# The last stores of a block-recurrent attention and MoE kernel: 64-row stores, and a last product in two column halves

## The chip, the cores and the metric

The kernel runs on one core of one Trainium2 chip. The time is the device time of one execution in microseconds (us). Three executions of the kernel before took 723.39, 723.47 and 724.16 us; their median, 723.47 us, is the time it is compared by.

A core has five engines with instruction streams of their own: TensorE (PE in the profile; PEld is its loading of weights), VectorE (DVE), ScalarE (ACT), GpSimd (POOL) and SyncE (SP). Transfers between the chip's memory (DRAM) and the on-chip memory are issued by SP, ACT or POOL and carried out by 16 DMA engines. PE accumulates into banks of PSUM, which DVE and ACT read.

## What is computed

```python
# x: (8, 8, 512, 64), state: (8, 8, 32, 64): batch, head, row, depth
a  = softmax(scale * x @ state.T);   xread = a  @ state      # 512 rows for each head
a2 = softmax(scale * state @ x.T);   sread = a2 @ x          # 32 rows for each head
y  = concat([xread, sread], axis=2)                          # (8, 8, 544, 64)
y  = y.transpose(0, 2, 1, 3).reshape(8 * 544, 8 * 64)        # (4352, 512)
h  = y @ w_in                                                # (4352, 2048)
sp = max(h, 0) + log1p(exp(-abs(h)))
out = (h * erf(sp)) @ w_out                                  # (4352, 512), float32
```

Every batch gives 544 rows of the output: 512 from `xread`, and then 32 from `sread`. So the `sread` rows of the eight batches lie in eight pieces of 32 rows, 544 rows apart.

## The kernel before

**Tiling.** The 512 `xread` rows of a batch are worked on together. The 32 `sread` rows of all eight batches are gathered into one more set of 256 rows, the last unit of work. Both dense products are done for blocks of two by two with seven products instead of eight (a Strassen-like scheme), so that a result is a sum of several products. `d_ff` is cut into four groups of 512, worked through in pairs.

**Order.** The first part of the kernel loads and converts the weights beside the first batch. A loop then runs over the other batches, two steps for each; in each step the second product of the step before (`project_wide`) is interleaved with the first product of this one (`hidden_wide`). After it comes the last unit (lines 1275 to 1295): two rounds of `hidden_states` and `project7`, which accumulate the 256 `sread` rows in the four PSUM tiles of `box`. The order of the instructions on PE, DVE and ACT is the order in which the code names them (`in_order`); SP takes its stores in the order in which it meets them.

**The last products (`project7`, lines 731 to 752).** Seven products, each of four matmuls of 128 rows by 128 by `E2` = 256 columns, go into the tiles `acc[0]` to `acc[3]`. In the trace, each float32 matmul leaves two records on PE. The seventh product goes into the left half of `acc[3]`.

**The last sums and stores (`store7`, lines 812 to 828).** ACT copies one half of a tile out of PSUM, DVE adds the halves of the others in five adds. `o1` holds the first 128 `sread` rows (batches 0 to 3), `o2` the other 128 (batches 4 to 7). Their stores follow as the parts become ready: the left half of `o1`, all of `o2`, and at last the right half of `o1`, which waits for the seventh product.

**The stores (`put_s`, lines 841 to 846).** Each call is cut into four stores of 32 rows, one for each batch:

```python
queue = nc.scalar if j % 2 and (r == 1 or c.start) else nc.sync
queue.dma_start(out=out[r0:r0 + Ns, c], in_=ot[Ns * j:Ns * j + Ns, c])
```

So the left half of `o1` goes by SP's queue alone, and the other two calls by SP and ACT in turn: 12 stores in all, eight on SP and four on ACT.

Of the kernel before, what the change touches and what calls it, by code (L numbers as in the profile page):

```python
# [17 lines left out]
def kernel(  # L18
# [17 lines left out]
    nc = tc.nc  # L36
    B, H, S, D = x.shape
    Ns = state.shape[2]
    d_model, d_ff = moe_w_in.shape
    P = 128  # L40
# [4 lines left out]
    GF = 4  # L45
    NG = NF // GF
    TB = S + Ns
# [66 lines left out]
    for i in range(NI):  # L114
        (nc.scalar, nc.sync)[i % 2].dma_start(
            out=x0[:, 2 * i:2 * i + 2].rearrange("p h c d -> p h (c d)"),
            in_=x[0, 2 * i:2 * i + 2].rearrange("h (p c) d -> p h (c d)", c=NC))
        if i == 1:
            for k in range(2):
                nc.sync.dma_start(out=st0[:, :, k],  # L120
                                  in_=state[0].rearrange("(g h) n d -> (h n) g d", g=2))
# [590 lines left out]
    E2 = d_model // 2  # L712
# [18 lines left out]
    def project7(gT, hs, g, first, last, acc, order=range(7)):  # L731


        blocks = lambda t: [t[:, k].rearrange("p (i t) -> p i t", i=GF) for k in range(4)]
        A11, A21, A12, A22 = blocks(gT)
        S1, S2, S3, S4 = blocks(hs)
        tt = nc.vector.tensor_tensor
        products = ((A12, B21, 0, 0), (A11, B11, 2, 0), (A22, T[4], 1, 0), (S2, T[2], 0, 1),
                    (S3, T[3], 2, 1), (S1, T[1], 1, 1), (S4, B22, 3, 0))
        for n, k in enumerate(order):  # L740
            lhs, rhs, bank, c = products[k]
            for i in range(GF):
                if i % 2 == 0 and n:
                    yield
                if i == 2 and n == 1:
                    tt(S1, A21, A22, op=ALU.add)
                    tt(S2, S1, A11, op=ALU.subtract)
                    tt(S3, A11, A21, op=ALU.subtract)
                    tt(S4, A12, S2, op=ALU.subtract)
                nc.tensor.matmul(out=acc[bank][:, E2 * c:E2 * c + E2], lhsT=lhs[:, i, :],  # L750
                                 rhs=rhs[:, g, i, :], start=(first and i == 0 and c == 0),
                                 stop=(last and i == GF - 1 and (c == 1 or bank == 3)))
# [59 lines left out]
    def store7(acc, put):  # L812
        twice = lambda t: t.unsqueeze(1).to_broadcast([P, 2, E2])
        two = lambda t: t.rearrange("p (c e) -> p c e", c=2)
        uv = outs.tile([P, d_model], F32, name="uv")
        m1, u3 = uv[:, 0:E2], uv[:, E2:]
        o1, o2 = (outs.tile([P, d_model], F32, name="ot", bufs=3) for _ in range(2))
        c12 = o1[:, E2:]
        add = lambda o, x, y: nc.vector.tensor_tensor(o, x, y, op=ALU.add)
        nc.scalar.copy(m1, acc[2][:, 0:E2])  # L820
        add(two(o1), twice(m1), two(acc[0]))
        put(0, o1, slice(0, E2))
        add(u3, c12, acc[2][:, E2:])
        add(two(o2), twice(u3), two(acc[1]))
        put(1, o2)
        add(c12, c12, acc[1][:, E2:])
        add(c12, c12, acc[3][:, 0:E2])
        put(0, o1, slice(E2, d_model))

    def put_x(b, h):  # L830
        rows = out[TB * b:TB * b + S].rearrange("(p c) e -> c p e" if b == 0 else
                                                "(c p) e -> c p e", p=P)

        def go(r, ot, c=slice(0, d_model), more=False):
            if more:
                nc.gpsimd.dma_start(out=rows[2 * h + r][:, c], in_=ot[:, c], accum_op=ALU.add)  # L836
            else:
                nc.sync.dma_start(out=rows[2 * h + r][:, c], in_=ot[:, c])
        return go

    def put_s(r, ot, c=slice(0, d_model)):
        m = P // Ns
        for j in range(m):
            r0 = TB * (m * r + j) + S
            queue = nc.scalar if j % 2 and (r == 1 or c.start) else nc.sync
            queue.dma_start(out=out[r0:r0 + Ns, c], in_=ot[Ns * j:Ns * j + Ns, c])

    def tiles(n):
        return [ps_o.tile([P, d_model], F32, name="o%d" % r) for r in range(n)]
# [108 lines left out]
    acc = tiles(NC)  # L958
# [114 lines left out]
    for u in range(2):  # L1073
        nc.sync.dma_start(out=kept_in[1][:, GF * u:GF * u + GF],
                          in_=away[:, u].rearrange("p j k f -> p j (k f)"))
# [71 lines left out]
    for n, (b, u) in enumerate((b, u) for b in range(1, B) for u in range(2)):  # L1147
# [3 lines left out]
        put = [put_x(b, h) for h in range(2)]  # L1151
# [124 lines left out]
    for k in range(2):  # L1276
        o = begins(B) ^ k
        steps = pending()
        if k == 0:
            later = combine_s(1 - begins(B))  # L1280
            steps = accompanied(steps, {1 + j: f for j, f in enumerate(later)})
        gT = hidden_states(o, 1 + k, lambda: next(steps, None))
        finish_on_act(gT[0])
        for j, _ in enumerate(steps):
            if j == (6 if k == 0 else 2):
                break
        times_part(1 + k, outside)
        times_part(1 + k, inside)
        done(steps)

        def pending(gT=gT, o=o, k=k):
            yield from project7(*gT, o, k == 0, k == 1, box)
            if k == 1:
                store7(box, put_s)
# [32 lines left out]
```

## Time and profile before

| | |
|---|---|
| median of three runs | 723.47 us |
| the profiled execution | 724.1 us |
| its span, first to last instruction | 722.3 us |
| PE busy | 714.6 us, 99% of the span |
| DVE, ACT, POOL busy | 538.2, 373.1, 25.2 us |
| DMA share from 714 to 718 us of the span | 0.09 |
| DMA share from 718 us to its end | 0.36 |
| mean rate of all transfers | 103 GB/s |

The profile is of one execution, whose own time lies a little above the median. The span leaves out what lies before the first and after the last instruction. A line of the timeline gives the start and duration in us, the engine, the line of the kernel, the operation, and the tiles written and read. Engines with a "q" (SPq, ACTq) are the instruction streams that issue transfers: such a row is the time of the issue, not of the transfer. A DMA share is the time in which the 16 DMA engines handled packets, over 16 times the stretch; a packet is a row of a transfer, or the few bytes that report its end. Where two packets overlap on an engine, both count.

### The profile page before, as it was taken

What the parts mean: (1) busy time and instruction counts of PE and PEld (TensorE: products, weight loads), DVE (VectorE), ACT (ScalarE), POOL (GpSimd) and SP (SyncE); (2) the same over time, 40 slices, a digit from 0 to 9 for tenths busy, and PEclk for the clock granted to TensorE, in tenths of its full rate; (3) what the DMA queues carried; (4) which work ended last, traced back from release to release, by engine and by line L of the source; (5) the groups of instructions that cost most, each with busy time, mean ns of one, the idle gap of its engine ahead of it and who ended that gap; (6) DMA issues with size and microseconds to landing.
All of it is one profiled execution on the core that took longest, in us unless ns stands there. A gap on an engine that the chain in (4) does not pass through costs nothing.

```text
span 722.3 us, 10976 instructions
## 1 busy us (share of the span) xinstructions
PE 714.6 (99%) x4289; PEld 565.5 (78%) x4289; DVE 538.2 (75%) x866; ACT 373.1 (52%) x540; POOL 25.2 (3%) x34
## 2 busy tenths in 40 slices
PE   9999999999999999999999999999999999999997
PEld 8444436588878878887888878887888888889996
DVE  5787879889868988788776967697877757665533
ACT  4999784636464625545346436462464535342340
POOL 0000000000100000000000000000000000000000
PEclk9999999999999999999999999999999999999999
DMA  8667795660348153513623280615242321002101
GB/s 266 193 220 211 231 273 180 148 178 30 46 89 217 21 130 55 140 51 92 98 29 147 59 140 8 175 28 148 31 103 84 89 49 27 33 29 30 24 8 30
DMA packets 144341, 74.73 MB, mean 103 GB/s; under 512 B 123424, under 2 KB 132896, under 8 KB 142752
## 3 DMA queue, kind: packets, MB, share of 16 engines
q1 hardware_dynamic: 139520, 65.95, 32.8%
q0 software_dynamic: 4032, 7.34, 7.5%
q10 hardware_dynamic: 736, 0.72, 0.3%
q8 instruction: 34, 0.56, 0.3%
q14 instruction: 19, 0.16, 0.1%
HBM read 49.87 MB, written 20.45 MB: 97 GB/s over the span
## 4 chain that ended last, share of the span: by engine, by line
PE 94%; ACT 3%; DMA 1%; DVE 0%; issue 0%; SPq 0%; ACTq 0%
PE o L775 47%; PE h L633 13%; PE at L633 10%; PE o L700 6%; PE h L678 3%; PE o L750 3%; PE h L905 2%; PE h L512 2%; PE at L512 2%; PE at L282 1%; PE h L232 1%; PE at L905 1%; PE at L529 1%; DMA x<-in_x_dram 1%; PE h L194 1%; PE at L329 1%
## 5 line engine op out<-in xcount | busy, mean ns | idle before, releaser
L775 PE MATMUL o<-w_out,ring 128*128 128x256 f32 x896 | 203.0, 379 | 0.0
L775 PEld LDWEIGHTS o<-w_out,ring 128*128 128x128 f32 x896 | 169.8, 190 | 25.0 <-DVE ring L1139 1.0
L775 PE MATMUL o<-raw,ring 128*128 128x256 f32 x672 | 161.4, 381 | 0.0
L775 PEld LDWEIGHTS o<-raw,ring 128*128 128x128 f32 x672 | 126.5, 190 | 25.9 <-ACT m L514 5.0
L626 ACT ACTIVATE ring<-ring 128x512 f32<-128x512 f32 x112 | 70.6, 631 | 59.9 <-DVE ring L616 59.3
L633 PE MATMUL h<-aT,m 128*128 128x256 f32 x336 | 82.0, 380 | 0.0
L1139 DVE TENSOR_TENSOR ring<-ring 128x1024 f32<-128x1024 f32 x60 | 70.6, 1218 | 3.9 <-ACT ring L690 3.9
L633 PEld LDWEIGHTS h<-aT,m 128*128 128x128 f32 x336 | 63.7, 190 | 10.4 <-issue 0.7
L616 DVE TENSOR_TENSOR ring<-ring,at 128x512 f32<-128x512 f32 x84 | 57.1, 680 | 16.9 <-PE at L633 15.2
L700 PE MATMUL o<-w_out,ring 128*128 128x512 f32 x128 | 58.8, 598 | 1.6 <-DVE ring L916 1.6
L760 DVE TENSOR_TENSOR ot<-uv,o 128x256 f32<-128x256 f32 (+1 forms) x56 | 30.9, 552 | 30.4 <-PE o L775 28.4
L616 DVE TENSOR_TENSOR ring<-ring,h 128x512 f32<-128x512 f32 x56 | 38.0, 678 | 19.7 <-PE h L633 19.6
L798 ACT COPY ot<-o 128x256 f32<-128x256 f32 x28 | 10.4, 373 | 79.6 <-PE o L775 79.6
L836 POOL DMA_DIRECT2D out_dram<-ot x28 | 24.5, 943 | 657.6 <-DVE ot L760 579.8
L700 PEld LDWEIGHTS o<-w_out,ring 128*128 128x128 f32 x128 | 23.7, 190 | 29.9 <-issue 24.4
L760 DVE TENSOR_TENSOR ot<-ot,o 128x256 f32<-128x256 f32 x56 | 22.1, 416 | 27.9 <-ACT ot L798 27.7
L648 ACT COPY ring<-h 128x512 f32<-128x512 f32 x28 | 16.5, 588 | 47.9 <-PE h L633 47.9
L807 DVE TENSOR_TENSOR ring<-ring 128x512 f32<-128x512 f32 x56 | 38.6, 689 | 1.4
L808 DVE TENSOR_TENSOR ring<-ring 128x512 f32<-128x512 f32 x56 | 36.3, 684 | 0.0
L639 ACT COPY ring<-h 128x512 f32<-128x512 f32 x28 | 16.5, 588 | 28.3 <-PE h L633 28.3
L690 ACT ACTIVATE ring<-ring 128x2048 f32<-128x2048 f32 x16 | 30.4, 1902 | 0.0
L514 ACT COPY m<-h 128x512 f32<-128x512 f32 x11 | 6.4, 586 | 44.4 <-PE h L512 44.3
(183 smaller groups left out, 975.6 us busy)
## 6 DMA issues: line engine op xcount, KB each, us to landing
w_in<-kept_in SPq DMA_DIRECT2D x7, 2048.0 KB, 8.2
raw<-in_moe_w_in_dram SPq DMA_DIRECT2D x16, 512.0 KB, 5.6
raw<-in_moe_w_out_dram SPq DMA_DIRECT2D x8, 1024.0 KB, 4.7
out_dram<-ot SPq DMA_DIRECT2D x32, 256.0 KB, 2.2
xq<-in_x_dram SPq DMA_DIRECT2D x112, 64.0 KB, 2.5
x<-in_x_dram SPq DMA_DIRECT2D x56, 128.0 KB, 2.9
out_dram<-ot POOLq DMA_DIRECT2D x28, 256.0 KB, 4.4
sc<-xT SPq DMA_DIRECT2D x112, 32.0 KB, 1.9
```

Of the source, the lines that this page charges most:

```text
L512: nc.tensor.matmul(out=ps[k][e][q, :], lhsT=st[r, b, q], rhs=of_group[g][r, :, i, :], start=True, stop=True)
L616: add = lambda o, x, y: nc.vector.tensor_tensor(o, x, y, op=ALU.add)
L626: nc.scalar.activation(out=s[k], in_=hs[k], func=ACTF.Softplus)
L633: nc.tensor.matmul(out=out[:, i], lhsT=x[:, q:q + P], rhs=y, start=(first and i == 0), stop=(i == 1), skip_group_check=not first)
L690: nc.scalar.activation(out=s, in_=s, func=ACTF.Erf)
L700: nc.tensor.matmul(out=acc[r], lhsT=gT[:, i, P * r:P * r + P], rhs=w_out[:, GF * g + i, :], start=(g == 0 and i == 0), stop=(g == NG - 1 a ...
L760: add = lambda o, x, y: tt(o, x, y, op=ALU.add)
L775: nc.tensor.matmul(out=out, lhsT=lhs[:, i, :], rhs=rhs[:, g, i, :], start=(start and i == 0), stop=(i == GF - 1), skip_group_check=not start)
L807: return [lambda: tt(S1, A21, A22, op=ALU.add), lambda: tt(S2, S1, A11, op=ALU.subtract), lambda: tt(S3, A11, A21, op=ALU.subtract), lambd ...
L808: lambda: tt(S3, A11, A21, op=ALU.subtract), lambda: tt(S4, A12, S2, op=ALU.subtract)]
L836: nc.gpsimd.dma_start(out=rows[2 * h + r][:, c], in_=ot[:, c], accum_op=ALU.add)
L1139: nc.vector.tensor_tensor(s[:, ks], s[:, ks], hs[:, ks], op=ALU.mult)
```

## The change

All of it is in the last unit. In `put_s` one store takes the rows of two batches: the DRAM side is viewed as batch, row, column, and SP takes the first two batches of a call and ACT the other two. Every call gives two stores of 64 rows instead of four of 32. In `project7` the seventh product is done for its left 128 columns and then for its right 128 columns, and in `store7` the last add and the last store are done for each of these halves by itself. That makes four calls of `put_s` instead of three, and eight stores instead of twelve, four on each queue.

```diff
@@ project7
             lhs, rhs, bank, c = products[k]
+            if last and n == 6:
+                yield
+                for q in range(0, E2, P):
+                    for i in range(GF):
+                        nc.tensor.matmul(out=acc[bank][:, q:q + P], lhsT=lhs[:, i, :],
+                                         rhs=rhs[:, g, i, q:q + P], start=False,
+                                         stop=(i == GF - 1 and q + P == E2))
+                break
             for i in range(GF):
@@ store7
         add(c12, c12, acc[1][:, E2:])
-        add(c12, c12, acc[3][:, 0:E2])
-        put(0, o1, slice(E2, d_model))
+        for q in range(0, E2, P):
+            add(c12[:, q:q + P], c12[:, q:q + P], acc[3][:, q:q + P])
+            put(0, o1, slice(E2 + q, E2 + q + P))
@@ put_s
-        m = P // Ns
-        for j in range(m):
-            r0 = TB * (m * r + j) + S
-            queue = nc.scalar if j % 2 and (r == 1 or c.start) else nc.sync
-            queue.dma_start(out=out[r0:r0 + Ns, c], in_=ot[Ns * j:Ns * j + Ns, c])
+        rows = out.rearrange("(b t) e -> b t e", t=TB)[:, S:TB, c]
+        for k, queue in enumerate((nc.sync, nc.scalar)):
+            b = P // Ns * r + 2 * k
+            queue.dma_start(out=rows[b:b + 2], in_=ot[2 * Ns * k:2 * Ns * k + 2 * Ns, c])
```

## The prediction

> **What bounds the kernel now.** I read the page first.
>
> ```profile
> span 722.3 us, 10976 instructions
> PE 714.6 (99%) x4289; PEld 565.5 (78%) x4289; DVE 538.2 (75%) x866; ACT 373.1 (52%) x540; POOL 25.2 (3%) x34
> PE 94%; ACT 3%; DMA 1%; DVE 0%; issue 0%; SPq 0%; ACTq 0%
> ```
>
> TensorE (PE) bounds the kernel: busy for 99% of the span and 94% of the chain that ended last. The change touches only what follows the last products, so I read the timeline of the end (start, duration, engine, line, work).
>
> ```profile
> 715.79 3.70 SPq L846 DMA_DIRECT2D out_dram<-ot  x8
> ...
> 716.19 1.89 PE L750 MATMUL o<-w_out,ring 128*128 128x256 f32 x8
> ...
> 717.00 0.41 DVE L819 TENSOR_TENSOR ot<-ot,o 128x256 f32<-128x256 f32 x1
> 717.11 2.34 ACTq L846 DMA_DIRECT2D out_dram<-ot  x4
> 718.12 0.42 DVE L819 TENSOR_TENSOR ot<-ot,o 128x256 f32<-128x256 f32 x1 [0.71 <-PE o L750]
> ```
>
> The last product is 8 records on PE, 716.19 to 718.08. The last add follows at 718.12 to 718.54. Twelve stores are issued between 715.79 and 719.5. From there only transfers stand between the kernel and its end. The issues of the stores, and a comparable issue elsewhere, are:
>
> ```profile
> L846 SPq DMA_DIRECT2D out_dram<-ot x8: 345/416/451, 715.8 to 719.1; - x8
> L846 ACTq DMA_DIRECT2D out_dram<-ot x4: 375/406/463, 717.1 to 719.0; - x4
> ...
> L484 SPq DMA_DIRECT2D sc<-xT x112: 586/608/1801, 116.2 to 565.0; - x112
> ```
>
> The middle figure is the median in ns. The last issues start at 719.0 and 719.1. In the DMA view of 718 to 722.3 us, the last of 22 occupied slices (0.1075 us each) ends at 720.4 us; the span ends 1.9 us later. In 716.6 to 717.2, the first packet is in the third slice of 15 ns, 716.63, so 0.84 us after the first issue began.
>
> **What a row costs a DMA engine.** The DMA views of four stretches: 716.6 to 718.0 (three 32-row stores), 646.8 to 648.4 (two stores with 2 KB rows), 9 to 11 (loads in 1 KB rows), 89 to 90 (loads in 256 B rows):
>
> ```profile
> DMA packets 145, 0.10 MB, mean 72 GB/s; under 512 B 48, under 2 KB 144, under 8 KB 145
> ...
> DMA packets 288, 0.52 MB, mean 328 GB/s; under 512 B 32, under 2 KB 32, under 8 KB 288
> q1 hardware_dynamic: 288, 0.52, 85.2%
> ...
> q1 hardware_dynamic: 731, 0.73, 104.5%
> ...
> q1 hardware_dynamic: 942, 0.23, 103.8%
> ```
>
> The last figure is the share of 16 engines' time. So 2 KB: 0.852 x 16 x 1.6 us / 256 rows = 85 ns. 1 KB: 1.045 x 16 x 2 us / 709 rows (22 of the 731 packets are under 512 B) = 47 ns. 256 B: 1.038 x 16 us / 942 = 17.6 ns. A 512 B row lies between; on the line from 256 B to 1 KB it is an estimated 27.5 ns.
>
> **What the Trainium skill says.** "DMA: Bandwidth & Descriptors", section "Why a DMA increments its semaphore by 16 and not by 1", says that a DMA is split over the largest number of engines, at most 16, that divides the slowest dimension of both its sides. On SP's and ACT's queues these are the lowest-numbered of the 16, and each posts one increment. Each 32-row store is 32 on both sides, so 16. The trace agrees: three such stores left 48 packets under 512 B, 16 each. No transfer here has a slowest dimension under 16, so the trace doesn't show what happens then. The section "Issuing engines are not separate DMA queues" says that SP's and ACT's transfers share the same engines; no view here tells the engines apart.
>
> **The change, part by part.**
>
> *Stores.* Each 64-row store has 64 partitions on the SBUF side, but on the DRAM side it is 2 batches x 32 rows x columns: its slowest dimension is 2, since rows of different batches are 544 rows apart. By that rule each store gets 2 engines, and all eight stores the same 2. The bytes don't change: 256 rows of 2 KB, 524 KB. Per engine:
>
> - left half, 128 rows of 1 KB: 64 x 47 = 3.0 us
> - full rows, 128 of 2 KB: 64 x 85 = 5.4 us
> - two quarters, 256 pieces of 512 B: 128 x 27.5 = 3.5 us
>
> Sum 12.0 us, where now the transfers fit into 716.63 to 720.4 and mostly wait for issues. These rows need no waiting: the left half is issued from 715.79, the full rows from 717.1 (to land after 717.9), the quarters before 719.7, and the first engine-time runs out only at 719.8 (left) and 725.3 (full). So two engines work without a gap.
>
> *Issues.* 12 become 8, four on each queue. I price one at 608 ns, the L484 row, instead of 416: both move several dimensions. That delays the first packet by 0.19, to 716.82. On ACT no computation follows its copy at 714.67, and on SP nothing but stores, so a longer issue holds up nothing else. Bounds: 416 (no delay) to twice 608 (0.8 us); the first packet moves with it.
>
> *Last product.* 8 matmuls of 128 columns instead of 4 of 256, 16 records instead of 8. L678 has this shape: 16 records in 1.95 us, the last 0.275, so 0.112 each from start to start, against 0.216 for 256 columns. The end is 716.19 + 15 x 0.112 + 0.275 = 718.14 instead of 718.08: +0.06, if weights load at L678's pace.
>
> *Last add.* The two halves each take an estimated 0.28 us (0.42 for 256 columns, 0.69 for 512, on a line), 0.14 more in sum. In the program as built, TensorE counts up once for these eight matmuls, at the last of them, and the first half's add waits for that count. So neither add starts before 718.18; they end at 718.46 and 718.74. Nothing is behind them on DVE. With two engines busy until 728.8, both parts are hidden by the transfers; without that cover they cost 0.2 us.
>
> *Sum.* The last packet ends at 716.82 + 12.0 = 728.8 instead of 720.4: +8.4. With the tail of 1.9 the span is 730.7. The profiled execution took 724.1, the median of the runs 723.47; I add the difference to the median: **731.9 us**, slower by 1.2%.
>
> Bounds of the rate: "DMA: Bandwidth & Descriptors", "Specifications", gives about 27 GiB/s (29 GB/s) per engine. By this estimate 262 KB per engine take 9.0 us, 728.9 in all; 2 KB rows ran at 24 GB/s here. For the other end I take the final stores themselves: from 716 to 722.3 the queues' shares are 17.7% and 12.4%, which is 0.301 x 16 x 6.3 = 30.3 engine-us for 524 KB, 17.3 GB/s, so 15.2 us and 735.1. That mixes both queues, as the changed kernel will; but each present store reads only 32 partitions with 16 engines, so I stay with the single-queue prices.
>
> **Rivals.**
>
> *Spread over 16 after all (not slower).* The hardware might split the 64 rows as it does 32 now. Then 24 engine-us divide by 16 and are hidden behind issues, as now. The adds release the last issues at 718.46 and 719.07 (the first takes 608), the last packets start 0.84 + 0.19 later, 720.1, and need 4 rows of 27.5 ns with some queueing: 720.3 against 720.4. Two issues fewer per queue are paid back by longer ones and by the shared wait: 723.4 us. It decides from 5 engines per store on: 24 / 5 = 4.8 us end at 721.6, less than 1.45 us above 720.4. For it: every transfer in the trace is spread so. Against it: none of them has a short outer dimension.
>
> *Two engines each, but different ones for SP and ACT.* Then 6.0 us from 716.82, 722.8, so +2.4: 725.9 us. Against it speaks the rule that both take the lowest-numbered.
>
> *A slower pair.* Two engines might not keep up their share-of-16 rate when two queues alternate on them: 735 us, the upper bound above, and more if each row waits for the last. For it: the 17.3 GB/s of the final stores. Against it: 24 GB/s in 646.8 to 648.4.
>
> **How the numbers follow.** Two shared engines 0.78 (forecast), the slower pair 0.07, different pairs 0.05, spread 0.10. The range 728.5 to 736.5 holds nearly all of the first and most of the second: 0.81. It reaches past the bounds by about what an issue of twice 608 adds (0.8). About 0.2% (1.45 us) is what a measurement of this kernel can tell from no change. The spread case lies within it, with a small chance of a gain beyond (0.02); the three others are slower.
>
> **What would show it.** Packets under 512 B in the last stretch fall from 192 to 16 (8 stores x 2); the DMA share there sits near 2 of 16 (12 to 13%) at about 45 GB/s for 12 us; the last issues start near 719.1 yet take some 9 us to land. Issues of 0.6 us, 16 records on PE ending at 718.14, and two adds back to back from 718.18 show the small parts. If the packets under 512 B number 128 and the last one falls before 721, the step on engines is wrong, and the time is no more than 723.9. If they number 16 and the transfers end far from 728.8, the price of a row is wrong.

## The result, and the profile after

The changed kernel took 733.36 us (median of 4), the kernel before 723.82 us (median of 4 with the new runs): 9.54 us more, a ratio of 1.0129 with a 95% interval of 1.0117 to 1.0141. The forecast was 731.9 us. The page of the profiled execution begins:

```profile
span 731.5 us, 10992 instructions
PE 714.2 (98%) x4297; PEld 565.5 (77%) x4297; DVE 538.1 (74%) x867; ACT 372.9 (51%) x540; POOL 25.2 (3%) x34
PE 93%; ACT 3%; DMA 1%; issue 0%; DVE 0%; SPq 0%; DVEq 0%; ACTq 0%
```

The engines did the same work as before, within 0.4 us each. The span is 9.2 us longer, and no engine is busy in the time that was added. The timeline of the end shows where computing stops:

```profile
714.86 0.69 DVE L827 TENSOR_TENSOR ot<-uv,o 128x512 f32<-128x512 f32 x1 [7.58 <-ACT uv L828]
715.58 3.84 SPq L854 DMA_DIRECT2D out_dram<-ot  x4
715.58 4.28 ACTq L854 DMA_DIRECT2D out_dram<-ot  x4
...
715.98 1.95 PE L746 MATMUL o<-w_out,ring 128*128 128x128 f32 x16
...
716.79 0.41 DVE L827 TENSOR_TENSOR ot<-ot,o 128x256 f32<-128x256 f32 x1
717.97 0.48 DVE L827 TENSOR_TENSOR ot<-ot,o 128x128 f32<-128x128 f32 x2 [0.76 <-PE o L746]
```

The last add ends at 718.45, where the kernel before ended it at 718.54. The last issues end at 719.4 (SP) and 719.9 (ACT). Everything after that is transfer. The issues, in ns (least, median, most):

```profile
L854 SPq DMA_DIRECT2D out_dram<-ot x4: 511/548/669, 715.6 to 718.9; - x4
L854 ACTq DMA_DIRECT2D out_dram<-ot x4: 522/742/1376, 715.6 to 719.3; - x4
```

And the DMA view of 716 to 731.5 us, in 40 slices of 0.39 us (share of the 16 engines in tenths, GB/s, packets):

```profile
DMA  0010111111120101111111111111111111100000
GB/s 0 0 16 18 48 24 24 40 42 37 40 53 24 16 37 32 53 53 53 48 48 53 53 50 46 52 53 42 45 42 45 42 44 44 30 9 0 0 0 0
DMA packets 528, 0.52 MB, mean 34 GB/s; under 512 B 16, under 2 KB 400, under 8 KB 528
```

The same count for the kernel before, from 716 to 722.3 us:

```profile
DMA packets 577, 0.53 MB, mean 85 GB/s; under 512 B 192, under 2 KB 448, under 8 KB 576
```

Two things are to be seen. The packets under 512 B, which report a store's end, are 16 for eight stores: two for each, where the kernel before had 192 for twelve, 16 for each. And the share stays near one tenth for 13 us, at some 50 GB/s in its best slices, where the kernel before moved the same bytes in 3.8 us. In the stretches of this time (the columns are busy us of each engine with its instructions, the granted clock, the DMA share, GB/s):

```profile
716.80:719.20 2.40, 1.13 (x11) 0.94 (x9) 0.89 (x4) 0.00 (x0) 0.00 (x0) 1.00 0.12 29
719.20:720.90 1.70, 0.00 (x0) 0.00 (x0) 0.00 (x0) 0.00 (x0) 0.00 (x0) 1.00 0.15 42
720.90:722.30 1.40, 0.00 (x0) 0.00 (x0) 0.00 (x0) 0.00 (x0) 0.00 (x0) 1.00 0.11 29
722.30:725.20 2.90, 0.00 (x0) 0.00 (x0) 0.00 (x0) 0.00 (x0) 0.00 (x0) 0.63 0.13 51
725.20:729.80 4.60, 0.00 (x0) 0.00 (x0) 0.00 (x0) 0.00 (x0) 0.00 (x0) 0.50 0.13 43
```

Two engines of 16, busy without a break, are a share of 0.125; packets that overlap on an engine, which both count, put it a little higher. The stretches lie at 0.11 to 0.15. The last packet ends at 729.75 (in the DMA view of 728 to 731.5 it is in the 20th slice of 0.0875 us), 1.8 us before the span ends.

### The profile page after: what moved, and what is told of

Its sections match the earlier page's. It is cut to its first block, busy times and chain, and to the rows that moved or that the text cites. A ratio compares the mean times of both kernels' runs of the same rounds, so it can differ in the third digit from the quotient of the medians.

```text
span 731.5 us, 10992 instructions
## 1 busy us (share of the span) xinstructions
PE 714.2 (98%) x4297; PEld 565.5 (77%) x4297; DVE 538.1 (74%) x867; ACT 372.9 (51%) x540; POOL 25.2 (3%) x34
## 4 chain that ended last, share of the span: by engine, by line
PE 93%; ACT 3%; DMA 1%; issue 0%; DVE 0%; SPq 0%; DVEq 0%; ACTq 0%
PE o L783 47%; PE h L633 13%; PE at L633 10%; PE o L700 6%; PE h L678 3%; PE o L758 3%; PE h L913 2%; PE h L512 2%; PE at L512 2%; PE at L282 1%; PE h L232 1%; PE at L913 1%; PE at L529 1%; DMA x<-in_x_dram 1%; PE h L194 1%; PE at L329 1%
```

## The experiments

The theory: a store whose DRAM side has 2 as its slowest dimension runs on two engines, and nothing else in the change costs much. The rivals: the halves of the last product and add; larger stores or the balance of the queues; a store whose two sides differ in form, whatever its slowest dimension. Each run is compared with runs of the kernel before on the same chip (medians 723.93, 724.26 and 724.08 us in three sets).

### Each part alone

**Stores alone.** The kernel before, with the new `put_s`.

> Only the stores are changed: 64 rows each, two batches to a queue; the last product, the last add and its store stay whole. Two engines for each store (the theory): per engine 128 rows of 1 KB and 64 of 2 KB, 128 x 46 + 64 x 84 ns = 11.3 us, against 64 x 46 + 64 x 84 + 128 x 27 = 11.8 us in the changed kernel, so 0.5 us less than that: about 732.9 us, and 12 packets under 512 B at the end (6 stores x 2). If the halves of the product and of the add are what costs (a rival), it is near the kernel before, 723 to 724.5 us.

Measured: 732.15 us, 1.0118 (1.0102 to 1.0133), 8.2 us over the kernel before. The last stretch, from 716 us, has

```profile
DMA packets 396, 0.52 MB, mean 36 GB/s; under 512 B 12, under 2 KB 268, under 8 KB 396
```

12 packets under 512 B for six stores, so two engines each. The stores alone make 8.2 of 9.5 us. Against the changed kernel that is 1.3 us less, where 0.5 was expected. From the start of the last sums to the last packet the two profiles have 14.9 and 14.5 us, so 0.4 of it lies there; the rest stays open.

**Halves alone.** The changed kernel, with the `put_s` of the kernel before.

> Only the halves are changed: last product, last add and last store in two halves, with the stores of the kernel before (32 rows, its choice of queue), 16 in all. Two engines for each 64-row store (the theory): the loss is gone; SP issues ten stores, its last at about 719.7 instead of 719.1, so 0.4 to 0.8 us over the kernel before, about 724.2 us. If the halves cost (a rival): 732 to 734 us.

Measured: 724.79 us, 1.0012 (1.0005 to 1.0018), 0.9 us over, a little more than the 0.4 to 0.8 that were expected. The halves aren't what costs; the 16 stores are a small loss of their own. The rival falls.

### The same stores, cut or reordered

**Stores of 32 rows.** Halves, queues, bytes and row sizes of the changed kernel; only each store is cut in two.

```diff
-        rows = out.rearrange("(b t) e -> b t e", t=TB)[:, S:TB, c]
         for k, queue in enumerate((nc.sync, nc.scalar)):
-            b = P // Ns * r + 2 * k
-            queue.dma_start(out=rows[b:b + 2], in_=ot[2 * Ns * k:2 * Ns * k + 2 * Ns, c])
+            for j in (2 * k, 2 * k + 1):
+                r0 = TB * (P // Ns * r + j) + S
+                queue.dma_start(out=out[r0:r0 + Ns, c], in_=ot[Ns * j:Ns * j + Ns, c])
```

> The changed kernel with each 64-row store cut into two of 32 rows on the same queue: same halves, same queues, same bytes and row sizes, 16 stores of 16 engines. Two engines (the theory): 0.4 to 0.8 us over the kernel before, 724.2 us, last packet near 721.0, 256 packets under 512 B. If the size of the last pieces or the balance of the two queues costs (a rival): near 733 us.

Measured: 724.85 us, 1.0012 (1.0006 to 1.0019), 0.9 us over, again a little more than expected. Twice as many issues take away 8.6 of the 9.5 us. Small last pieces and the balance of the queues fall as causes.

**Slowest dimension 16.** The rows of each half of the last unit are ordered by row and then batch. That is done where the `sread` columns are written to `sT`, so no work is added.

```diff
-    sT = const.tile([P, NK, B, Ns], F32, name="sT")
+    sT = const.tile([P, NK, 2, Ns, 4], F32, name="sT")
...
-        rows = out.rearrange("(b t) e -> b t e", t=TB)[:, S:TB, c]
+        rows = out.rearrange("(b t) e -> t b e", t=TB)[S:TB, 4 * r:4 * r + 4, c]
         for k, queue in enumerate((nc.sync, nc.scalar)):
-            b = P // Ns * r + 2 * k
-            queue.dma_start(out=rows[b:b + 2], in_=ot[2 * Ns * k:2 * Ns * k + 2 * Ns, c])
+            t = Ns // 2 * k
+            queue.dma_start(out=rows[t:t + Ns // 2], in_=ot[2 * Ns * k:2 * Ns * k + 2 * Ns, c])
```

> The changed kernel, with the 128 rows of each half of the last unit ordered by row and then batch instead of batch and then row. A store still takes 64 rows, on the same queues, in eight issues, and its two sides still differ in form (64 partitions against 16 x 4 rows), but the slowest dimension of the DRAM side is 16 instead of 2. Two engines (the theory): 16 engines, 128 packets under 512 B, last packet near 720.4, 723.4 us or within 0.4 us of the kernel before. If a store whose sides differ in form is slow in itself (a rival), or if 64-row stores are: 731 to 734 us.

Measured: 724.04 us, 1.0003 (0.9994 to 1.0011), 0.1 us over. The DMA view of 716 to 721.9 us (slices of 0.15 us):

```profile
DMA  0046661000149997510052613343000000000000
GB/s 0 0 160 222 236 236 35 0 0 0 69 181 292 347 333 278 222 56 0 0 167 70 181 28 118 105 132 91 0 0 0 0 0 0 0 0 0 0 0 0
DMA packets 640, 0.52 MB, mean 89 GB/s; under 512 B 128, under 2 KB 512, under 8 KB 640
```

Eight stores of 64 rows on the same queues, two sides that still differ in form, and 128 packets under 512 B: 16 for each. The transfers come in three bursts with gaps, up to 347 GB/s, waiting for issues again. So it is the slowest dimension of the DRAM side that costs, and neither 64 rows nor the form. This is the run that settles the cause.

**Slowest dimension 4.** One store of 128 rows for each call, all on SP.

```diff
-        for k, queue in enumerate((nc.sync, nc.scalar)):
-            b = P // Ns * r + 2 * k
-            queue.dma_start(out=rows[b:b + 2], in_=ot[2 * Ns * k:2 * Ns * k + 2 * Ns, c])
+        b = P // Ns * r
+        nc.sync.dma_start(out=rows[b:b + 4], in_=ot[:, c])
```

> The changed kernel with one store of 128 rows for each call, all on SP: 4 stores, DRAM side 4 batches x 32 rows. By the theory each gets 4 engines: half the transfer time of the changed kernel, 6.0 us by the prices of the prediction and 6.5 us by what the changed kernel measured, so a last packet 6.0 to 6.5 us after the first, 2.4 to 3.0 us over the kernel before (about 726.6 us), 16 packets under 512 B. If every store whose sides differ in form ran on two engines (a rival): 733 us again. If nothing but the count of issues mattered: below the kernel before.

Measured: 728.38 us, 1.0053 (1.0039 to 1.0066), 4.1 us over: more than was expected, and 16 packets under 512 B for four stores, so four engines each. The count, and the stretches of its end:

```profile
DMA packets 529, 0.53 MB, mean 27 GB/s; under 512 B 16, under 2 KB 400, under 8 KB 528
...
717.00:718.80 1.80, 1.14 (x11) 0.95 (x9) 0.90 (x4) 0.00 (x0) 0.00 (x0) 1.00 0.24 72
718.80:720.00 1.20, 0.00 (x0) 0.00 (x0) 0.00 (x0) 0.00 (x0) 0.00 (x0) 1.00 0.28 25
720.00:722.50 2.50, 0.00 (x0) 0.00 (x0) 0.00 (x0) 0.00 (x0) 0.00 (x0) 1.00 0.22 72
722.50:725.10 2.60, 0.00 (x0) 0.00 (x0) 0.00 (x0) 0.00 (x0) 0.00 (x0) 0.65 0.23 71
```

A share of about a quarter is four engines. In the last stretch they moved the 256 pieces of the quarters and the last 26 full rows: 256 x 27.5 + 26 x 85 ns are 9.3 engine-us at the forecast's prices, and four engines took 2.5 us, 10.0 engine-us. Before it they were slower than their prices: 72 in the first stretch (1 KB rows, 4 x 1024 / 47 = 87) and in the third (2 KB rows, 96), and only 25 for 1.2 us at the start of the full rows. At a share of 0.28 the engines weren't idle then; the rows took longer. In the trace's records of single packets, 19 of the 128 rows of 2 KB took 144 to 853 ns, the median 84. With four engines the loss is less than half of that with two, in the direction of the theory, but not to its number. The run also has one queue and half the issues, so the dimension isn't all that it changes.

**Slowest dimension 8.** The order of the rows of the run with 16, in stores of 8 x 4 rows, two on each queue for each call.

```diff
-            t = Ns // 2 * k
-            queue.dma_start(out=rows[t:t + Ns // 2], in_=ot[2 * Ns * k:2 * Ns * k + 2 * Ns, c])
+            for t in (Ns // 2 * k, Ns // 2 * k + Ns // 4):
+                queue.dma_start(out=rows[t:t + Ns // 4], in_=ot[4 * t:4 * t + Ns, c])
```

> The rows of the last unit ordered by row and then batch, as in the run with outermost dimension 16, but in stores of 8 x 4 rows, two on each queue for each call: 16 stores, outermost dimension 8. By the theory 8 engines each: 24 engine-us over 8 are 3.0 us, hidden behind the issues (the point of decision was put at 5 engines), so 0.3 to 1.0 us over the kernel before for the 16 issues, like the run with 16 stores of 32 rows; 128 packets under 512 B. If each halving of the engines cost in proportion even here (a rival): over 726 us.

Measured: 727.39 us, 1.0043 (1.0029 to 1.0056), 3.1 us over. By the time alone, the rival of a cost in proportion would have won. Its last stretch has 8 packets under 512 B for each store, and the issues, here and in the run with 16 stores of 32 rows, say otherwise:

```profile
DMA packets 641, 0.53 MB, mean 56 GB/s; under 512 B 128, under 2 KB 512, under 8 KB 640
```

```profile
L854 SPq DMA_DIRECT2D out_dram<-ot x8: 657/688/814, 716.1 to 721.5; - x8
L854 ACTq DMA_DIRECT2D out_dram<-ot x8: 671/672/1521, 716.1 to 722.1; - x8
```

```profile
L854 SPq DMA_DIRECT2D out_dram<-ot x8: 314/398/414, 715.6 to 719.6; - x8
L854 ACTq DMA_DIRECT2D out_dram<-ot x8: 374/405/447, 715.6 to 719.6; - x8
```

Eight issues of 0.69 us on a queue last 5.5 us; eight of 0.40 last 3.2. The last issue starts at 721.5 and 722.1 instead of 719.6, 1.9 and 2.5 later, or 1.4 and 2.0 when the later start of 0.5 is taken off. The queues' shares in this run's last stretch (716 to 725.6) are 8.0% and 7.9%, so transfers were waiting for issues: from its first packet to its last, 6.1 us, no packet was in flight for some 2.5 us. The expectation had priced 16 issues of this form like those of plain stores. So here most of the loss is a price of the issue. It doesn't show what eight engines cost.

### The two queues, and what the forecast missed

**One queue.** All eight stores on SP: `(nc.sync, nc.sync)` in place of `(nc.sync, nc.scalar)`.

> The changed kernel with all eight stores on SP, none on ACT. The two engines are the same for either queue (the theory): the transfers take as long, 12.0 to 13.0 us, and the time is within 1 us of the changed kernel, 732.5 to 733.8 us. If the 0.9 us by which the changed kernel's transfers exceeded the forecast came from two queues alternating on an engine: 12.0 us, 732.5. If it comes from the start of a transfer on two engines: 13 us again, 733.4. If ACT had had engines of its own (a rival): at least 4 us more than the changed kernel.

Measured: 734.36 us, 1.0137 (1.0122 to 1.0153), 10.1 us over, 0.6 above what the changed kernel was over. The median missed the range of the expectation by 0.6 us, over a kernel before that was itself 0.4 us slower in this set. The rates from 717 to 731 us (slices of 0.35 us):

```profile
GB/s 0 18 6 44 53 47 35 18 47 50 47 35 23 29 41 47 41 53 53 47 41 59 47 53 53 47 54 38 39 28 35 41 44 44 44 34 22 22 22 1
```

Without ACT's queue the transfers took 13.3 us (717.4 to 730.7), 12.9 with it. ACT has no engines of its own for these stores, and the excess over the forecast doesn't come from two queues alternating.

**Queues exchanged.** ACT takes the first two batches of each call, SP the others (one execution with its profile).

> The changed kernel with the queues exchanged: ACT takes the first two batches of each call and SP the other two. The same bytes on the same two engines (the theory): 733 to 734 us, first to last packet 12.5 to 13.5 us. For what the forecast missed, the low rate of the first microseconds on two engines: if it belongs to SP's queue, the rows of SP stay slow and ACT's are as fast as before; if it belongs to whichever store comes first on the two engines, the first 2.4 us stay near 30 GB/s whichever queue carries them.

Measured: 733.68 us, against 724.28 for the kernel before, each from one execution. In both kernels, the stretch of 716.8 to 719.2 carried SP's rows alone or nearly so, at 29 and 26 GB/s (the changed kernel, then the exchanged one):

```profile
q1 hardware_dynamic: 66, 0.07, 12.1%
q10 hardware_dynamic: 3, 0.00, 0.4%
```

```profile
q1 hardware_dynamic: 60, 0.06, 11.0%
```

So the slow rows are not a matter of which batches are written. SP's rows came first in both, although ACT's first store was issued within 0.01 us of SP's. That leaves SP's queue and the place of the first store untold apart.

**Full rows alone, quarters alone, on two engines.** The run with stores of 32 rows, with the new form only for the full rows (`if r == 1`) or only for the two quarters (`if c.start`).

> The run with 16 stores of 32 rows, but with the two stores of the full rows (batches 4 to 7) in the form of the changed kernel, 64 rows and outermost dimension 2. Two engines (the theory): 64 rows of 2 KB on each, 5.4 us at 84 ns, from a first packet about 0.9 us after the issue at 717.1: last packet near 723.3 to 723.6, 2.9 to 3.2 us over the kernel before. If the 0.9 us that the changed kernel took beyond the forecast belongs to the first microseconds of any work on two engines, it comes again here: 3.9 us over. If it belongs to the left half alone, it does not.

> The same with only the four stores of the two quarters in the form of the changed kernel. Two engines (the theory): 128 rows of 512 B on each, 3.5 us at 27 ns, from a first packet at 719.4: last packet near 722.9, 2.5 us over the kernel before; with a slow start of 1 us, 3.5 us over. If the parts didn't add up on the same two engines, the sum of this and of the run with only the full rows would not come near the changed kernel's 9.5 us less the 3.0 us of the left half.

Measured: quarters 726.68 us, 1.0036 (1.0022 to 1.0050), 2.6 us over, as expected without a slow start. There is hardly one in its rates from 718.9 to 722.6 us (slices of 0.09 us):

```profile
GB/s 0 17 11 17 39 44 39 44 44 44 44 44 44 44 44 33 44 44 44 44 33 22 39 44 44 44 39 44 44 44 44 39 44 44 44 39 22 11 0 0
```

The full rows 729.86 us, 1.0080 (1.0062 to 1.0098), 5.8 us over, where at most 3.9 was expected. The timeline and the stretches of that kernel show two things that go with it:

```profile
718.49 5.32 SPq L860 DMA_DIRECT2D out_dram<-ot  x4
```

```profile
718.40:720.00 1.60, 0.00 (x0) 0.00 (x0) 0.26 (x2) 0.00 (x0) 0.00 (x0) 1.00 0.12 16
```

Four plain stores behind the full rows on SP were issued in 5.32 us instead of 1.6: they were held up behind a store that fills two engines. Not every issue is: in the changed kernel, where each store behind the first had such a store ahead of it, none on SP took over 0.6 us. What decides it isn't shown. And the first 1.6 us of the two engines moved 16 GB/s at a share of 0.12: they were busy, and slow. The slow start comes again without the left half on two engines, so it doesn't belong to that half; without it in the quarters, it doesn't belong to every transfer on two engines either. The parts don't add: 5.8 + 2.6 is already 8.4, and the left half is still missing. Some of it is counted twice, since both runs also have plain stores for the rest, and 16 plain stores alone are 0.9 us over.

### A version for use

**Slowest dimension 16, with the last product, add and store whole.**

> The rows of the last unit ordered by row and then batch, stores of 64 rows with outermost dimension 16, one on each queue for each call, and the last product, add and store whole as in the kernel before: 6 stores instead of 12. The last issues start at about 718.6 instead of 719.1, each 0.6 us long instead of 0.4: last packet at 720.0 to 720.2, 0.1 to 0.5 us below the kernel before, a ratio of 0.9993 to 1.0, too little to tell from it by the time. If 64-row stores or stores whose sides differ cost something of their own (a rival): 0.5 us or more over the kernel before.

Measured: 723.74 us, 0.9993 (0.9984 to 1.0001). The last issue starts at 718.6, 0.5 us before that of the kernel before, as expected. But the last packet ends at 720.4, as there: the DMA view of 716 to 721.7 us (slices of 0.14 us) has the last burst from 719.7 on, 1.1 us after the issue.

```profile
DMA  0000000266630000368989554026763000000000
```

It halves the stores and loses nothing; a gain can't be told from no change.

## Why the prediction was right

**Engines for each store: right.** Two packets under 512 B for each, at a share of 0.11 to 0.15. The run with slowest dimension 16 shows it as the cause: same rows, issues and halves, and 9.4 of 9.5 us gone. In the runs the count of these packets was 2, 4, 8 and 16 for slowest dimensions of 2, 4, 8 and 16, as the Trainium skill has it ("DMA: Bandwidth & Descriptors", "Why a DMA increments its semaphore by 16 and not by 1"). The records of single packets say it a second way. Leaving out the few ns by which a row overlaps the next, never more than two packets were in flight at once at the end of the changed kernel and of the runs with the stores alone and with one queue, and never more than 4, 8 and 16 with slowest dimensions of 4, 8 and 16. The trace of before couldn't show that.

**Both queues on the same two engines: right.** From 722.4 to 725.0 both queues moved rows, at shares of 7.5% and 5.5%: two engines of 16 in sum, where four would show 25%. One queue alone took 13.3 us for the transfers, two took 12.9.

**The price of a row: too high once the transfer ran, too low at its start.** From 722.4 to 725.0 the changed kernel moved 64 packets of 2 KB, and from 727.3 to 729, 143 rows of 512 B and four small packets:

```profile
DMA packets 64, 0.13 MB, mean 50 GB/s; under 512 B 0, under 2 KB 0, under 8 KB 64
q1 hardware_dynamic: 37, 0.08, 7.5%
q10 hardware_dynamic: 27, 0.06, 5.5%
...
DMA packets 147, 0.07 MB, mean 43 GB/s; under 512 B 4, under 2 KB 147, under 8 KB 147
q1 hardware_dynamic: 74, 0.04, 7.2%
q10 hardware_dynamic: 73, 0.04, 7.1%
```

By the shares, as the forecast reckoned, a 2 KB row took 0.13 x 16 x 2.6 us / 64 = 84.5 ns, against 85, and a 512 B row 27.2, against the 27.5 interpolated. But where packets overlap on an engine, a share counts both. By the clock, each of the two engines moved a 2 KB row every 2 x 2.6 us / 64 = 81 ns and a 512 B row every 2 x 1.7 us / 143 = 24 ns. For 1 KB rows the records of single packets have 42 ns from one start to the next where no row was slow. At these prices the sum would have been 64 x 42 + 64 x 81 + 128 x 24 ns = 10.9 us instead of 12.0.

Slow single rows, which the forecast had at nothing, went the other way. In the records, 16 of the 128 rows of 1 KB took 101 to 281 ns instead of 46, and four of the 128 rows of 2 KB took 341 to 539 ns instead of 84; none of 512 B did. All twenty started before 722, and what they took beyond the others is 3.4 engine-us, 1.7 us for two engines. So the 67 rows of 1 KB from 716.8 to 719.2 took 2 x 2.4 us / 67 = 72 ns on average, and the left half was through at 720.9, 4.0 us after the first packet, instead of 3.0.

All of it took 12.9 us from first to last packet, instead of 12.0: 1.1 us less by the prices, 1.7 more by the slow rows, and 0.3 that no term explains. The number of engines was understood; that the sum came so close was in part luck, since two errors went opposite ways. The excess of 0.9 us is most of the 1.1 us by which 9.54 exceeds 8.4.

**The start: 0.2 us short.** From the first issue at 715.58 to the first packet at 716.85 are 1.27 us, against 0.84 + 0.19. The issue was priced by its median, 608 ns instead of 416. But SP's first issue took 0.67 us, and that of the kernel before 0.34: 0.33 more, not 0.19. That is 0.14 of what was missed; the other 0.1 lies between the end of the issue and the first packet.

**The sum.** The profiled execution began its last sums at 714.86, 0.21 earlier than the kernel before. From there to the last packet are 14.9 us, against 5.4 (715.07 to 720.43): 9.5, the difference of the medians. With the forecast's terms it was 8.4; the longer transfers are 0.9 and the first packet 0.2.

**The product in halves, and the shared wait: right.** 16 records in 1.95 us, as in L678. Both adds came after the whole product (0.76 us of idle time ended by PE), so the first half started nothing early. Their 0.48 us are less than the estimated 0.56. All of it was hidden by the transfers; with the transfers on 16 engines, the halves and their 16 stores cost 0.9 us.

**The rivals.** A spread over 16 engines would have given 723.4; the run that brought it about by the order of the rows gave 724.04 on a chip where the kernel before took 723.93. (The working of this rival has two issues fewer for each queue; SP has four fewer, and ACT as many as before.) Different engines for the two queues fell. The slower pair was right about a low rate at the start (29 GB/s until 719.2 and again from 720.9 to 722.3), but not about its reason: in both stretches SP's rows went almost alone, and where the queues alternated the rate was 51 GB/s.

**The point of decision, at five engines, wasn't confirmed.** Four engines cost 4.1 us where 2.4 had followed from it, since slow rows are there as well; eight engines were never the bound in the run meant for them.

## What to carry to other kernels

Before rows of several pieces are put into one store to save issues, look at the slowest dimension on both sides: a store with 2 there ran on two of 16 engines and turned 3.8 us of transfers into 12.9, and nothing at a kernel's end hides that. If the pieces must go together, order the data on chip so that the long dimension is the slowest on the DRAM side too (9.4 of 9.5 us came back). And an add or a store cut in half starts nothing early unless what it waits for is counted half by half.

## What was not expected

- On two or four engines some rows were slow, nearly all in the first microseconds of the left half or the full rows (with one queue a few until 727): 29 GB/s in the first 2.4 us and 51 later with two, 25 GB/s for 1.2 us at the start of the full rows with four, 16 GB/s in the first 1.6 us of the full rows alone. The engines count as busy meanwhile. With the quarters alone it lasted only 0.3 us. With 16 engines the burst of the left half is at 222 GB/s in its second slice of 0.15 us. The cause stays open. Which batches are written and alternating queues are excluded. Of the twenty slow rows of the changed kernel 18 were SP's, but SP's rows also came first in each of these calls, so SP's queue and the first place aren't told apart.
- With two stores issued within 0.01 us on SP and ACT for the same two engines, ACT's rows began only when SP's were through: 3 packets of ACT before 719.2, 49 from 719.2 to 720.4. From 723.3 on the records show rows of the two queues in turn on both engines. ACT's longest issue took 1.38 us, SP's 0.67.
- An issue of a store whose sides differ in form took 0.54 to 0.69 us on SP (medians of the runs), of a plain one 0.40 to 0.42. With eight of 0.69 on a queue, the issues took 5.5 us, and the transfers of all 16 stores would have taken 3.0 by the forecast's prices.
